# Attention into two expert layers on one core: softplus of the first two steps and two weight loads listed with the attention, the inverse root in 8 instructions, and new orders where the second layer changes group and ends

## The chip, the core and the metric

One core of a Trainium2 chip runs the whole program. Its engines have their own instruction streams: TensorE (PE, matrix products into PSUM), VectorE (DVE), ScalarE (ACT), GpSimd (POOL) and SyncE (SP, which issues the DMAs). An engine takes its instructions in the order in which the program lists them, and one that waits holds all that stands behind it. The metric is device time in microseconds of one execution, the median of several.

## The reference

Attention over 4 batches, 8 heads, 576 positions of 64, then an expert layer with softplus, then a gated one with a root mean square norm:

```
cum    = cumsum(max(s, 0))
scores = q k^T / 8 + min(-(cum_i - cum_j), 0), causal
x      = softmax(scores) v                      # to 2304 tokens x 512
h      = x @ w_in;  g = softplus(h);  x = g @ w_out         # d_ff 2048
xn     = x / sqrt(mean(x*x) + 1e-6) * rms_g
out    = (silu(xn @ w_gate) * (xn @ w_val)) @ w_out2        # d_ff 1536
```

q, k, v, s and rms_g are 32-bit floats; the weight matrices arrive as 64-bit floats.

## The kernel before

Every product that needs 32-bit accuracy is done as three matmuls of a high and a low part (hi x hi, hi x lo, lo x hi). A high part is a rounded copy made by ScalarE; the low part is what is left, a subtraction on VectorE or GpSimd. A 64-bit weight chunk of 128 x 512 is loaded (`w_fetch`, L227, tile raw), and turned into 32 bits by ScalarE (`w_conv_a`, L238), VectorE (`w_conv_d`, L245 to L249) and GpSimd (`w_conv_p`, L261), then split.

The attention runs in 16 pairs of heads. It is written as a list of small operations with engines, durations and dependences (`attention_ops`); `attention_order` picks them greedily by a table of ranks (OFF), and the order so found is that of every engine. At its end stand the last pairs' products with v (V0, V1, Z0, Z1, L552), the copies of their results (O0 to O2, `a_ox`, L590, tile xz), their way over memory and the division (BC on SyncE, XM on GpSimd, XW on SyncE, tile x, L614), and H0 and H1, the first two `m1_h` of the next layer.

The first expert layer (m1) runs in 96 steps: 6 tiles of 384 tokens by 16 chunks of d_ff. Step i has 12 matmuls into h (`m1_h`, L792 to L794), softplus twice on ScalarE (`m1_sp`: l, L813, and its rounded copy gh, L814), the low part on VectorE (`m1_gl`, gl, L818) and 12 matmuls into four banks y (`m1_y`, L830). TensorE's order is h(i+2), Y(i), h(i+3), Y(i+1). The other instructions are put at positions in units of a step (`at`, tables OFF1 and OFF2) and sorted. After a tile's last step its y is added to what was stored (`m1_evac`, L845), squared and summed (`m1_ss`: squares on ScalarE, L863, sums on GpSimd, L865), and the inverse root is made by `m1_inv` (L885): an integer seed and three Newton steps of three VectorE instructions each (L894, L896, L898) for all 384 tokens on 128 partitions; GpSimd then multiplies (L902). The sixth tile's inverse root lies in the second layer's first part.

The second layer (m2) runs in 36 calls of `m2_g`: 3 groups of 768 tokens by 12 chunks of d_ff (f = 0 to 11). Each call makes the products of a Strassen-Winograd scheme, named by their weight form and token form, in this order: A12 B21 (bank D), A11 B11 (bank A), S2 T2 (A), S1 T1 (D), S3 T3 (A), S4 B22 (D), A22 T4 (A). Each is six matmuls of 384 columns (L979 to L981). Between them stand two halves of nine matmuls of 512 columns of the chunk before (`m2_out`, L1071). What reads a bank between two products holds the next one that writes it: c1 (L1011), u2 (L1030), m5 (L1038) on ScalarE, vB (L1047) and gB (L1049) on VectorE. The token forms of a new group (tile xf) are split by `n_split`: the copy on ScalarE (L968), the subtraction (L970) on VectorE for one half of them and on GpSimd for the other. This is done in the last call of a group (B21, B11, T2) and in the first call of the next (`fresh`: T1, T3, B22, T4). There the six output banks of the old group are also copied (`m2_evac`, L1082 on ScalarE, L1084 on VectorE) and stored; three in the first call and three in the second one. `m2_end` does the last chunk.

Of the kernel before, what the change touches and what calls it, by code (L numbers as in the profile page):

```python
# [115 lines left out]
    "H0": -23.02,  # L116
    "H1": -64.43,
# [28 lines left out]
def attention_moe_kernel(ctx, tc, q, k, v, s, w_in, w_out, w_gate, w_val, w_out2, rms_g, out):  # L146
# [470 lines left out]
    def attention_ops():  # L617
# [90 lines left out]
        for i in range(2):  # L708
            op((f"H{i}", 0), "PE", 2.1, lambda i=i: m1_h(i),
               [(f"X{a}", 0) for a in range(KD)] + [("MT", NP - 1), ("CL", NA - 1), ("CP", len(CONV) - 1)] + [("R" + x, p) for x in "abcd" for p in (NP - 2, NP - 1)], NP, mode="f")  # L710
# [98 lines left out]
    def m1_sp(i):  # L809
        h = st.pop(("h", i))  # L810
        l = st["l", i] = m1_tile("l", 2)
        gh = st["gh", i] = m1_tile("gh", 3, F32R)
        nc.scalar.activation(out=l, in_=h, func=AF.Softplus)  # L813
        nc.scalar.activation(out=gh, in_=h, func=AF.Softplus)  # L814

    def m1_gl(i):
        gl = st["gl", i] = m1_tile("gl", 3, F32R)
        nc.vector.tensor_tensor(out=gl, in0=st.pop(("l", i)), in1=f32(st["gh", i]), op=ALU.subtract)  # L818
# [66 lines left out]
    def m1_inv(t, k):  # L885
# [4 lines left out]
        if k == 0:  # L890
            nc.vector.tensor_scalar(out=z.bitcast(I32), in0=ms.bitcast(I32), scalar1=-0.5, scalar2=1597463007.0,
                                    op0=ALU.mult, op1=ALU.add)
        elif k % 3 == 1:
            nc.vector.tensor_tensor(out=w, in0=z, in1=z, op=ALU.mult)  # L894
        elif k % 3 == 2:
            nc.vector.scalar_tensor_tensor(out=w, in0=w, scalar=-0.5, in1=ms, op0=ALU.mult, op1=ALU.mult)  # L896
        else:
            nc.vector.scalar_tensor_tensor(out=z, in0=w, scalar=1.5, in1=z, op0=ALU.add, op1=ALU.mult)  # L898
# [62 lines left out]
    def n_split(g, j, nm):  # L961
# [7 lines left out]
        eng = nc.gpsimd if g > 0 and i % 2 else nc.vector  # L969
# [22 lines left out]
    def m2_g(n, fill=None):  # L992
# [18 lines left out]
        act(out=c1, in_=A, func=AF.Copy)  # L1011
        if n:
            m2_hi(n - 1, 1)
            m2_lo(n - 1, 1)
        tt(out=gA, in0=D, in1=c1, op=ALU.add)
        act(out=s0, in_=gA, func=AF.Sigmoid)
        tt(out=s0, in0=gA, in1=s0, op=ALU.mult)
        if f == 1 and g > 0:
            m2_evac(g - 1, 1)
        if n:  # L1020
            m2_out(n - 1, 0)
        else:
# [8 lines left out]
        renew(fresh, "B22")  # L1031
# [55 lines left out]
    def m2_end():  # L1087
        n = NS2 - 1
        m2_out(n - 1, 1)
        m2_hi(n, 1)  # L1090
        m2_lo(n, 1)
        m2_out(n, 0)
        m2_evac(NG - 1, 0)
        m2_out(n, 1)
        m2_evac(NG - 1, 1)


    with tc.manual_schedule():
# [22 lines left out]
        with ExitStack() as es0:  # L1121
# [27 lines left out]
            for v in sorted({STEPS[i][0] for i in NS}):  # L1149
# [17 lines left out]
                for a in range(KD):  # L1167
                    at(e + OFF2["ss"] + OFF2["sr"] * a, m1_ss, t, a)
# [5 lines left out]
                for k in range(10):  # L1174
# [60 lines left out]
```

## Time and profile before

| | us |
|---|---|
| median of 3 runs (1060.23 to 1061.2) | 1060.93 |
| the profiled execution | 1059.71 |
| its span, from the first to the last instruction | 1057.9 |
| TensorE busy | 1029.3 (97%) |
| VectorE busy | 693.4 (66%) |
| GpSimd busy | 570.0 (54%) |
| ScalarE busy | 540.6 (51%) |

The attention takes roughly the first 221 us of the span, the first expert layer the next 400, the second one the rest. A row of the timeline gives the start, the busy time of a group of like instructions, the engine, the line, the operation, what it writes and reads, and in brackets the engine's idle time just before with what ended it. A matmul shows as busy from its start to its modelled end, and the next one starts before that end.

### The profile page before, as it was taken

How to read it: one execution, taken by the hardware profiler on the slowest of the kernel's cores; microseconds unless marked ns; L12 is line 12 of the kernel's file. 1: busy time of each engine (PE TensorE's matmuls, PEld its weight loads, DVE VectorE, ACT ScalarE, POOL GpSimd, SP SyncE). 2: the span in 40 equal slices, each digit the busy share in tenths (PEclk: the TensorE clock that was granted, in tenths of full speed). 3: DMA queues.
4: the chain of work that ended last, by engine and by line, in shares of the span. 5: the costliest groups of instructions: out<-in, count | busy, mean ns of one | idle time of the engine just before them, and what ended most of it. 6: DMA issues, size and time to landing. Idle time of an engine off the chain costs nothing.

```text
span 1057.9 us, 19448 instructions
## 1 busy us (share of the span) xinstructions
PE 1029.3 (97%) x7212; PEld 953.8 (90%) x7212; DVE 693.4 (66%) x1141; ACT 540.6 (51%) x1189; POOL 570.0 (54%) x477
## 2 busy tenths in 40 slices
PE   6999999999999999999999999999989999899997
PEld 5788877889999999999989998999979999799997
DVE  8888988418776756889898654545664346734444
ACT  2455666536656544544544544445554445644443
POOL 4378878736766433555767245355453433644331
PEclk9999999999999999999999999999999999999999
DMA  8367664345555575766542323224242233333221
GB/s 155 78 161 172 166 164 134 106 133 159 173 154 161 184 257 179 231 230 194 146 151 84 117 81 98 70 86 161 88 130 71 81 121 104 99 100 89 86 70 60
DMA packets 143758, 139.68 MB, mean 132 GB/s; under 512 B 68656, under 2 KB 118960, under 8 KB 143664
## 3 DMA queue, kind: packets, MB, share of 16 engines
q1 hardware_dynamic: 143632, 138.44, 44.5%
q8 instruction: 57, 0.93, 0.4%
q14 instruction: 37, 0.30, 0.1%
q0 software_dynamic: 32, 0.00, 0.0%
HBM read 106.73 MB, written 31.53 MB: 131 GB/s over the span
## 4 chain that ended last, share of the span: by engine, by line
PE 60%; DVE 7%; issue 3%; POOL 3%; DMA 2%; ACT 2%; SPq 0%; POOLq 0%; ACTq 0%; DVEq 0%
PE y L830 12%; PE o L1071 10%; PE A L979 4%; PE A L981 4%; PE A L980 4%; PE D L981 3%; PE D L979 3%; PE D L980 3%; PE h L792 3%; PE h L794 3%; PE h L793 3%; PE x L1071 2%; PE x L792 1%; PE x L794 1%; PE x L793 1%
## 5 line engine op out<-in xcount | busy, mean ns | idle before, releaser
L925 POOL TENSOR_TENSOR w<-wl,w 128x512 fp32r<-128x512 f32 x108 | 140.1, 1313 | 211.7 <-ACT w L924 211.7
L1071 PE MATMUL o<-w,gg 128*128 128x512 f32 x540 | 153.3, 393 | 0.3
L830 PE MATMUL y<-gh,w 128*128 128x384 f32 x768 | 149.8, 335 | 2.9 <-ACT gh L814 1.7
L830 PEld LDWEIGHTS y<-gh,w 128*128 128x128 f32 x768 | 134.4, 188 | 4.5 <-ACT gh L814 2.0
L1071 PEld LDWEIGHTS o<-w,gg 128*128 128x128 f32 x540 | 100.8, 188 | 19.4 <-ACT yt L1082 0.9
L979 PE MATMUL A<-xf,w 128*128 128x384 f32 x288 | 97.2, 338 | 6.2 <-DVE l L1047 4.7
L980 PE MATMUL A<-xf,w 128*128 128x384 f32 x288 | 96.9, 336 | 0.7 <-DVE xf L970 0.7
L981 PE MATMUL A<-xf,w 128*128 128x384 f32 x288 | 97.0, 337 | 0.0
L1047 DVE TENSOR_TENSOR l<-A,gh 128x384 f32<-128x384 f32 x36 | 20.0, 556 | 115.8 <-ACT w L924 113.3
L535 ACT ACTIVATE e<-t 128x448 f32<-128x448 f32 (+2 forms) x128 | 56.4, 505 | 71.3 <-PE t L528 66.4
L818 DVE TENSOR_TENSOR gl<-l,gh 128x384 fp32r<-128x384 f32 x96 | 79.3, 831 | 16.1 <-ACT gh L814 16.0
L261 POOL TENSOR_TENSOR wf<-ur 128x512 int32<-128x512 int32 x44 | 62.6, 1424 | 50.4 <-DVE ur L249 36.2
L485 DVE TENSOR_REDUCE mc<-s 128x2 f32<-128x512 f32 (+4 forms) x160 | 76.3, 534 | 19.0 <-PE s L470 15.0
L792 PE MATMUL h<-xh,w 128*128 128x384 f32 x256 | 85.6, 335 | 0.0
L793 PE MATMUL h<-xl,w 128*128 128x384 f32 x256 | 85.5, 334 | 0.0
L794 PE MATMUL h<-xh,w 128*128 128x384 f32 x256 | 85.5, 334 | 0.0
L830 PE MATMUL y<-gl,w 128*128 128x384 f32 x384 | 82.4, 335 | 2.3 <-DVE gl L818 2.2
L245 DVE TENSOR_SCALAR ur<-ur 128x512 f32<-128x512 f32 x68 | 51.3, 754 | 35.2 <-ACT ur L238 35.2
L979 PE MATMUL D<-xf,w 128*128 128x384 f32 x216 | 72.9, 338 | 0.0
L981 PE MATMUL D<-xf,w 128*128 128x384 f32 x216 | 72.8, 337 | 0.0
L980 PE MATMUL D<-xf,w 128*128 128x384 f32 x216 | 72.5, 336 | 0.0
L261 POOL TENSOR_TENSOR w<-ur 128x512 int32<-128x512 int32 x24 | 34.8, 1451 | 68.7 <-DVE ur L249 48.1
(171 smaller groups left out, 2662.8 us busy)
## 6 DMA issues: line engine op xcount, KB each, us to landing
wl<-wf SPq DMA_DIRECT2D x108, 256.0 KB
raw<-in_moe_w_out_dram SPq DMA_DIRECT2D x28, 512.0 KB
wf<-w SPq DMA_DIRECT2D x24, 512.0 KB
raw<-in_moe_w_in_dram SPq DMA_DIRECT2D x16, 512.0 KB
raw<-in_moe_w_gate_dram SPq DMA_DIRECT2D x12, 512.0 KB
raw<-in_moe_w_val_dram SPq DMA_DIRECT2D x12, 512.0 KB
xr<-x SPq DMA_DIRECT2D x28, 192.0 KB
qn<-in_q_dram SPq DMA_DIRECT2D x16, 288.0 KB
```

Of the source, the lines that this page charges most:

```text
L261: nc.gpsimd.tensor_tensor(out=w.bitcast(I32), in0=u, in1=r3, op=ALU.add)
L485: nc.vector.reduce_max(out=o, in_=x, axis=AX.X, negate=True)
L792: nc.tensor.matmul(o, wh, xh, start=start, stop=False)
L793: nc.tensor.matmul(o, wh, xl, start=False, stop=False)
L794: nc.tensor.matmul(o, wl, xh, start=False, stop=stop)
L818: nc.vector.tensor_tensor(out=gl, in0=st.pop(("l", i)), in1=f32(st["gh", i]), op=ALU.subtract)
L830: nc.tensor.matmul(y[m][:, 0:T], x[:, m * P:(m + 1) * P], r, start=first and x is w[0] and r is gh, stop=last and r is gl)
L925: nc.gpsimd.tensor_tensor(out=t[:, 1, 0:w], in0=src, in1=f32(t[:, 0, 0:w]), op=ALU.subtract)
L979: nc.tensor.matmul(o, wh[:, c], xh, start=first, stop=False, skip_group_check=True)
L980: nc.tensor.matmul(o, wh[:, c], xl, start=False, stop=False, skip_group_check=True)
L981: nc.tensor.matmul(o, wl[:, c], xh, start=False, stop=last, skip_group_check=True)
L1071: nc.tensor.matmul(st["o2"][m], x[:, m * P:(m + 1) * P], r, start=(f == 0 and k == 0), stop=(f == F2 - 1 and k == 2))
```

## The change

It has five parts.

Attention's end: H0 and H1 exchange their ranks and H1 follows H0. The softplus of both (SP0, SP1), their low parts (SG0, SG1) and two weight loads (FX, chunks 12 and 13) become operations of the attention's list. Their tiles come from pools that the attention has open.

Inverse root: the seed, then one Newton step and one step of third order, 8 instructions for 10. The two squares (k = 1 and 4) are ScalarE's; VectorE has the seed and five others. The sixth tile's squares of y are put into the second call of the second layer by hand.

Group changes: T1 is split at the end of the old group's last call, T3 right behind c1, both wholly on GpSimd; B22 wholly on VectorE, T4 one half on each, both right behind the silu. The six copies of the old group's banks are spread as (0, 1), (2), (3, 4) and (5), and VectorE has only banks 0 and 4 of them.

The first chunk's Y of the second layer's first call (`fill`) is put ahead of the sigmoid.

End: the last chunk's second half is finished before its first one, and the output banks are done one by one as 3, 4, 5, 0, 1, 2.

```
-    "H0": -23.02,
-    "H1": -64.43,
+    "H0": -64.43,
+    "H1": -23.02,
+    "SP0": -60.0,
+    "SP1": -60.0,
+    "SG0": -60.0,
+    "SG1": -60.0,
+    "FX": -60.0,
...
+               [(f"X{a}", 0) for a in range(KD)] + [("MT", NP - 1), ("CL", NA - 1), ("CP", len(CONV) - 1)] + [("R" + x, p) for x in "abcd" for p in (NP - 2, NP - 1)] + [("H0", 0)] * i, NP, mode="f")
+        for i in range(2):
+            op((f"SP{i}", 0), "ACT", 2.1 - 1.25 * i, lambda i=i: m1_sp(i), [(f"H{i}", 0)]
+               + [(f"E{x}{hd}", p) for x in "abcd" for hd in range(2) for p in (NP - 2, NP - 1)], NP)
+            op((f"SG{i}", 0), "DVE", 0.6, lambda i=i: m1_gl(i), [(f"SP{i}", 0)], NP)
+        for c in range(2):
+            op(("FX", c), "SP", 0.65, lambda c=c: w_fetch(1, NA + c), [("BC", NP - 1), ("CD", NA - 1)], NP)
...
     def m1_sp(i):
         h = st.pop(("h", i))
-        l = st["l", i] = m1_tile("l", 2)
-        gh = st["gh", i] = m1_tile("gh", 3, F32R)
+        if i < 2:
+            if "l01" not in st:
+                st["l01"] = pools["e"].tile([P, 2, 1600], F32, tag="e", name="l")
+                st["g01"] = pools["split"].tile([P, 4, S], F32R, tag="hl", name="g", bufs=3)
+            l, gh = st["l", i], st["gh", i] = st["l01"][:, i, 0:T], st["g01"][:, i, 0:T]
+        else:
+            l = st["l", i] = m1_tile("l", 2)
+            gh = st["gh", i] = m1_tile("gh", 3, F32R)
         nc.scalar.activation(out=l, in_=h, func=AF.Softplus)
         nc.scalar.activation(out=gh, in_=h, func=AF.Softplus)
 
     def m1_gl(i):
-        gl = st["gl", i] = m1_tile("gl", 3, F32R)
+        gl = st["gl", i] = m1_tile("gl", 3, F32R) if i > 1 else st["g01"][:, 2 + i, 0:T]
         nc.vector.tensor_tensor(out=gl, in0=st.pop(("l", i)), in1=f32(st["gh", i]), op=ALU.subtract)
...
-        elif k % 3 == 1:
-            nc.vector.tensor_tensor(out=w, in0=z, in1=z, op=ALU.mult)
-        elif k % 3 == 2:
-            nc.vector.scalar_tensor_tensor(out=w, in0=w, scalar=-0.5, in1=ms, op0=ALU.mult, op1=ALU.mult)
-        else:
-            nc.vector.scalar_tensor_tensor(out=z, in0=w, scalar=1.5, in1=z, op0=ALU.add, op1=ALU.mult)
+        elif k in (1, 4):
+            nc.scalar.activation(out=w, in_=z, func=AF.Square)
+        elif k in (2, 5):
+            nc.vector.scalar_tensor_tensor(out=w, in0=w, scalar=-0.1875 if k == 2 else 64.0 / 9.0, in1=ms, op0=ALU.mult, op1=ALU.mult)
+        elif k == 3:
+            nc.vector.scalar_tensor_tensor(out=z, in0=w, scalar=0.5625, in1=z, op0=ALU.add, op1=ALU.mult)
+        elif k == 6:
+            nc.vector.scalar_tensor_tensor(out=w, in0=w, scalar=-10.0 / 3.0, in1=w, op0=ALU.add, op1=ALU.mult)
+        else:
+            nc.vector.scalar_tensor_tensor(out=z, in0=w, scalar=5.0, in1=z, op0=ALU.add, op1=ALU.mult)
...
-        eng = nc.gpsimd if g > 0 and i % 2 else nc.vector
+        eng = nc.gpsimd if (g > 0 and i % 2 if pool is None else pool) else nc.vector
         eng.tensor_tensor(out=t[:, 1], in0=src, in1=f32(t[:, 0]), op=ALU.subtract)
...
-        def renew(go, *names):
+        def renew(go, *names, pool=(None, None)):
             if go:
                 for nm in names:
                     for j in range(2):
-                        n_split(g + ahead, j, nm)
+                        n_split(g + ahead, j, nm, pool[j])
+
+        def squares(k, *ks):
+            if n == k:
+                for a in ks:
+                    m1_ss(NTILE - 1, a)
 
         prod(D, n, "A12", "B21", True, True)
         prod(A, n, "A11", "B11", True, False)
         act(out=c1, in_=A, func=AF.Copy)
+        renew(fresh, "T3", pool=(1, 1))
         if n:
             m2_hi(n - 1, 1)
             m2_lo(n - 1, 1)
+        if f == 1 and g > 0:
+            m2_evac(g - 1, (5,))
         tt(out=gA, in0=D, in1=c1, op=ALU.add)
+        if n:
+            m2_out(n - 1, 0)
+        else:
+            fill()
+        if fresh:
+            m2_evac(g - 1, (0, 1))
         act(out=s0, in_=gA, func=AF.Sigmoid)
         tt(out=s0, in0=gA, in1=s0, op=ALU.mult)
-        if f == 1 and g > 0:
-            m2_evac(g - 1, 1)
-        if n:
-            m2_out(n - 1, 0)
-        else:
-            fill()
+        squares(1, 0, 1)
         renew(ahead, "B21", "B11")
-        renew(fresh, "T1", "T3")
+        renew(fresh, "B22", pool=(0, 0))
+        renew(fresh, "T4", pool=(0, 1))
...
-        renew(fresh, "T4")
+        squares(1, 2)
         if fresh:
-            m2_evac(g - 1, 0)
-        if n + 1 < NS2:
+            m2_evac(g - 1, (2,))
+        elif n + 1 < NS2:
             u_split(n + 1, (2, 3))
...
+        squares(1, 3)
+        if fresh:
+            u_split(n + 1, (2, 3))
+        if n == NS2 - 1:
+            tt(out=s1, in0=gB, in1=s1, op=ALU.mult)
+            tt(out=vB, in0=vB, in1=s1, op=ALU.mult)
...
-        m2_hi(n, 0)
-        tt(out=s1, in0=gB, in1=s1, op=ALU.mult)
-        m2_lo(n, 0)
-        tt(out=vB, in0=vB, in1=s1, op=ALU.mult)
-
-    def m2_out(n, h):
+        if n < NS2 - 1:
+            m2_hi(n, 0)
+            tt(out=s1, in0=gB, in1=s1, op=ALU.mult)
+            m2_lo(n, 0)
+            tt(out=vB, in0=vB, in1=s1, op=ALU.mult)
+        if fresh:
+            m2_evac(g - 1, (3, 4))
+        renew(ahead, "T1", pool=(1, 1))
...
-                if m % 2:
+                if m % 2 if g == NG - 1 else m not in (0, 4):
...
-        m2_out(n - 1, 1)
         m2_hi(n, 1)
         m2_lo(n, 1)
-        m2_out(n, 0)
-        m2_evac(NG - 1, 0)
-        m2_out(n, 1)
-        m2_evac(NG - 1, 1)
+        m2_hi(n, 0)
+        m2_lo(n, 0)
+        m2_out(n - 1, 1, (3, 4))
+        for m in (3, 4, 5, 0, 1, 2):
+            if m == 5:
+                m2_out(n - 1, 1, (5,))
+            m2_out(n, m // 3, (m,))
+            m2_evac(NG - 1, (m,))
...
-                    if (nm != "h" or i > 1) and (nm != "Y" or i + 1 < len(STEPS)):
+                    if (nm == "Y" or i > 1) and (nm != "Y" or i + 1 < len(STEPS)):
...
-                    at(x + OFF1[nm], fn, ph, c)
+                    if ph == 2 or c > NA + 1 or nm != "CF":
+                        at(x + OFF1[nm], fn, ph, c)
...
-                    at(e + OFF2["ss"] + OFF2["sr"] * a, m1_ss, t, a)
+                    if not x:
+                        at(e + OFF2["ss"] + OFF2["sr"] * a, m1_ss, t, a)
...
-                for k in range(10):
+                for k in range(8):
                     at(e + OFF2["iv" + x] + OFF2["in" + x] * (k + 1), m1_inv, t, k)
```

The list of ScalarE at the border between the attention and the first expert layer, before; l and gh are the softplus of a step, xz the attention's results on their way out, xh the next tokens' high part:

```order
L590 ACTIVATE xz<-x_4055 128x192 x2
L590 ACTIVATE xz<-o_4085 128x384
L590 ACTIVATE xz<-x_4094 128x192 x2
L590 ACTIVATE xz<-o_4111 128x384
L813 ACT_TABLE_LOAD
L813 ACTIVATE l<-h 128x384
L814 ACTIVATE gh<-h 128x384
L788 ACTIVATE xh<-xr 128x384
L813 ACTIVATE l<-h 128x384
L814 ACTIVATE gh<-h 128x384
L788 ACTIVATE xh<-xr 128x384
L813 ACTIVATE l<-x_4170 128x384
```

and of the changed kernel, from its table load on:

```order
L830 ACT_TABLE_LOAD
L830 ACTIVATE l<-h 128x384
L831 ACTIVATE g<-h 128x384
L595 ACTIVATE xz<-o_4033 128x384
L595 ACTIVATE xz<-o_4059 128x384
L595 ACTIVATE xz<-x_4045 128x192 x2
L830 ACTIVATE l<-h 128x384
L831 ACTIVATE g<-h 128x384
L595 ACTIVATE xz<-o_4091 128x384
L595 ACTIVATE xz<-x_4102 128x192 x2
L595 ACTIVATE xz<-o_4121 128x384
L799 ACTIVATE xh<-xr 128x384 x2
```

The softplus of step 0 stood behind every xz; now both of the first steps' softplus stand between them, and the table load ahead of all of them that are shown.

The list of VectorE in the first call of the last group, before; xf are split token forms, yt the copied output banks, `l<-A,gh` is vB and `gl<-gl` the silu:

```order
L1015 TENSOR_TENSOR gl<-D,gh 128x384
L1017 TENSOR_TENSOR gl<-gl 128x384
L970 TENSOR_TENSOR xf<-xs,xf 128x384 x3
L970 TENSOR_TENSOR xf<-acc,xf 128x384
L1084 COPY yt<-o 128x256 x4
L1047 TENSOR_TENSOR l<-A,gh 128x384
L1049 TENSOR_TENSOR gl<-D,gh 128x384
L1052 TENSOR_TENSOR gl<-A,gl 128x384
```

and now:

```order
L1044 TENSOR_TENSOR gl<-D,gh 128x384
L1122 COPY yt<-o 128x256 x2
L1052 TENSOR_TENSOR gl<-gl 128x384
L991 TENSOR_TENSOR xf<-xs,xf 128x384 x2
L991 TENSOR_TENSOR xf<-acc,xf 128x384
L1077 TENSOR_TENSOR l<-A,gh 128x384
L1079 TENSOR_TENSOR gl<-D,gh 128x384
L1088 TENSOR_TENSOR gl<-A,gl 128x384
```

Ahead of vB stood four splits and four copies; now it is three splits and two copies, and the copies stand ahead of the silu.

The list of GpSimd there, before; w are split weight forms, xf the token forms:

```order
L970 TENSOR_TENSOR xf<-xs,xf 128x384
L925 TENSOR_TENSOR w_11267<-wl,w_11267 128x512
L925 TENSOR_TENSOR w_11270<-xr,w_11270 128x256
L970 TENSOR_TENSOR xf<-xs,xf 128x384 x3
L925 TENSOR_TENSOR w_11371<-wl,w_11371 128x512
L925 TENSOR_TENSOR w_11374<-wl,w_11374 128x512
L970 TENSOR_TENSOR xf<-sq,xf 128x384
```

and now:

```order
L991 TENSOR_TENSOR xf<-xs,xf 128x384
L946 TENSOR_TENSOR w_11251<-wl,w_11251 128x512
L946 TENSOR_TENSOR w_11254<-xr,w_11254 128x256
L991 TENSOR_TENSOR xf<-xs,xf 128x384 x4
L991 TENSOR_TENSOR xf<-sq,xf 128x384
L946 TENSOR_TENSOR w_11373<-wl,w_11373 128x512
```

Three token forms, two weights and one token form (T4's) in a row have become four token forms and T4's with no weight between them.

## Rows read from the trace of the kernel before

**Rows 1.** the page, span, parts 1 and 2

```profile
span 1057.9 us, 19448 instructions
PE 1029.3 (97%) x7212; PEld 953.8 (90%) x7212; DVE 693.4 (66%) x1141; ACT 540.6 (51%) x1189; POOL 570.0 (54%) x477
```

**Rows 2.** timeline, TensorE, 224 to 227.5 us; start, us, group, count, idle before

```profile
224.81 1.67 PE L830 MATMUL y<-gh,w 128*128 128x384 f32 x8 [1.66 <-ACT gh L814]
226.31 0.85 PE L830 MATMUL y<-gl,w 128*128 128x384 f32 x4
227.01 0.33 PE L792 MATMUL h<-xh,w 128*128 128x384 f32 x1
```

**Rows 3.** timeline, ScalarE, 220 to 225 us

```profile
221.42 1.28 ACT L813 ACT_TABLE_LOAD   x1
```

**Rows 4.** timeline, SyncE, ScalarE and TensorE, 226 to 241 us

```profile
227.40 4.44 SPq L614 DMA_DIRECT2D x<-xz  x2
231.89 0.43 SPq L227 DMA_DIRECT2D raw<-in_moe_w_in_dram  x1
236.78 0.66 ACT L238 ACTIVATE ur<-raw 128x512 f32<-128x512 f32 x1 [6.62 <-DMA raw<-in_moe_w_in_dram]
239.62 0.96 PE L830 MATMUL y<-gl,w 128*128 128x384 f32 x4 [0.66 <-DVE gl L818]
```

**Rows 5.** busy time by stretch (us, then PE, PEld, DVE, ACT, POOL, clock, DMA)

```profile
484.00:556.00 72.00, 69.10 (x388) 66.80 (x387) 65.19 (x84) 35.74 (x75) 49.25 (x38) 1.00 0.53 166
```

**Rows 6.** timeline, TensorE, 494 to 549 us

```profile
495.14 0.79 PE L830 MATMUL y<-gl,w 128*128 128x384 f32 x3 [0.71 <-DVE gl L818]
503.61 0.62 PE L830 MATMUL y<-gh,w 128*128 128x384 f32 x2 [0.73 <-DVE yt L845]
539.68 0.79 PE L830 MATMUL y<-gl,w 128*128 128x384 f32 x3 [0.88 <-DVE gl L818]
547.35 1.28 PE L830 MATMUL y<-gh,w 128*128 128x384 f32 x3 [0.44 <-DVE yt L845]
```

**Rows 7.** VectorE by line and shape, 300 to 640 us; busy us, mean ns

```profile
L896 DVE SCALAR_TENSOR_TENSOR sh<-sh,sq 128x384 f32<-128x384 f32 x15 | 12.0, 802 | 0.3
L894 DVE TENSOR_TENSOR sh<-acc 128x384 f32<-128x384 f32 x15 | 11.1, 738 | 0.2
```

**Rows 8.** timeline, ScalarE and TensorE, 636 to 640 us

```profile
636.22 0.53 ACT L863 ACTIVATE acc<-yt 128x384 f32<-128x384 f32 x1 [1.41 <-POOL yt L902]
639.28 0.45 PE L979 MATMUL A<-xf,w 128*128 128x384 f32 x1 [1.47 <-ACT gh L1011]
```

**Rows 9.** timeline, VectorE, TensorE, GpSimd and ScalarE, the group changes

```profile
769.26 3.64 DVE L970 TENSOR_TENSOR xf<-xs,xf 128x384 fp32r<-128x384 f32 x3 [0.27 <-ACT xf L968]
774.39 1.41 DVE L1084 COPY yt<-o 128x256 f32<-128x256 f32 x4
775.72 0.54 DVE L1047 TENSOR_TENSOR l<-A,gh 128x384 f32<-128x384 f32 x1
771.67 0.45 PE L980 MATMUL A<-xf,w 128*128 128x384 f32 x1 [0.39 <-DVE xf L970]
776.41 0.41 PE L979 MATMUL A<-xf,w 128*128 128x384 f32 x1 [2.34 <-DVE l L1047]
783.85 0.47 PE L1071 MATMUL x<-w,gg 128*128 128x512 f32 x1 [0.31 <-DVE yt L1084]
919.02 0.41 PE L979 MATMUL A<-xf,w 128*128 128x384 f32 x1 [2.37 <-DVE l L1047]
770.13 2.36 POOL L970 TENSOR_TENSOR xf<-xs,xf 128x384 fp32r<-128x384 f32 x2 [0.22 <-PE o L1071]
773.41 0.65 ACT L1082 ACTIVATE yt<-o 128x256 f32<-128x256 f32 x2
```

**Rows 10.** timeline, SyncE, the end

```profile
1049.61 0.81 SPq L1085 DMA_DIRECT2D out_dram<-gl  x2
1054.45 0.90 SPq L1085 DMA_DIRECT2D out_dram<-yt  x2
```

More of the change, by code (lines that the diff above doesn't have):

```diff
@@ L709, in attention_ops @@
             op((f"H{i}", 0), "PE", 2.1, lambda i=i: m1_h(i),
-               [(f"X{a}", 0) for a in range(KD)] + [("MT", NP - 1), ("CL", NA - 1), ("CP", len(CONV) - 1)] + [("R" + x, p) for x in "abcd" for p in (NP - 2, NP - 1)], NP, mode="f")
+               [(f"X{a}", 0) for a in range(KD)] + [("MT", NP - 1), ("CL", NA - 1), ("CP", len(CONV) - 1)] + [("R" + x, p) for x in "abcd" for p in (NP - 2, NP - 1)] + [("H0", 0)] * i, NP, mode="f")
[5 more added lines that the diff above has]
+            op(("FX", c), "SP", 0.65, lambda c=c: w_fetch(1, NA + c), [("BC", NP - 1), ("CD", NA - 1)], NP)
         for o in ops:
@@ L959, in attention_moe_kernel, with n_split @@
     FORMS = ("B21", "B11", "T2", "T1", "T3", "B22", "T4")
-    def n_split(g, j, nm):
+    def n_split(g, j, nm, pool=None):
         i = FORMS.index(nm) + 7 * j
@@ L1014, in m2_g @@
             m2_lo(n - 1, 1)
+        if f == 1 and g > 0:
+            m2_evac(g - 1, (5,))
         tt(out=gA, in0=D, in1=c1, op=ALU.add)
-        act(out=s0, in_=gA, func=AF.Sigmoid)
-        tt(out=s0, in0=gA, in1=s0, op=ALU.mult)
-        if f == 1 and g > 0:
-            m2_evac(g - 1, 1)
         if n:
@@ L1023, in m2_g @@
             fill()
+        if fresh:
+            m2_evac(g - 1, (0, 1))
+        act(out=s0, in_=gA, func=AF.Sigmoid)
+        tt(out=s0, in0=gA, in1=s0, op=ALU.mult)
+        squares(1, 0, 1)
         renew(ahead, "B21", "B11")
-        renew(fresh, "T1", "T3")
+        renew(fresh, "B22", pool=(0, 0))
+        renew(fresh, "T4", pool=(0, 1))
         if n == N5:
@@ L1030, in m2_g @@
         act(out=u2, in_=A, func=AF.Copy)
-        renew(fresh, "B22")
         if n + 1 < NS2:
@@ L1053, in m2_g, with m2_out @@
         st["lt", n, 0], st["lt", n, 1] = s0, vB
-        m2_hi(n, 0)
-        tt(out=s1, in0=gB, in1=s1, op=ALU.mult)
-        m2_lo(n, 0)
-        tt(out=vB, in0=vB, in1=s1, op=ALU.mult)
-    def m2_out(n, h):
+        if n < NS2 - 1:
[6 more added lines that the diff above has]
+        renew(ahead, "T1", pool=(1, 1))
+    def m2_out(n, h, ms=None):
         f = n % F2
@@ L1064, in m2_out @@
         gh, gl = st["g", n]
-        ms = range(3 * h, 3 * h + 3)
+        ms = range(3 * h, 3 * h + 3) if ms is None else ms
         jobs = [(m, k) for k in range(3) for m in ms]
-        if n == NS2 - 1:
-            jobs = [(m, k) for m in ms for k in range(3)]
         for m, k in jobs:
@@ L1072, in m2_out, with m2_evac @@
                              stop=(f == F2 - 1 and k == 2))
-    def m2_evac(g, h):
+    def m2_evac(g, ms):
         W = DM // 2
-        for m in range(3 * h, 3 * h + 3):
+        for m in ms:
             r = 2 * T * g + m * P
```

## The prediction

> **What bounds the kernel now.** The page's busy shares come first: TensorE 97% of the span, no other engine above 66% [rows 1]. So the kernel is bound by the matmuls, and only what makes TensorE wait, or what lies ahead of its first and behind its last matmul, is worth time. The number of matmuls does not change. The second view is TensorE's timeline, read for rows with idle time in brackets. What such a row costs is worked out so: four matmuls of 384 columns take 0.85 us, one takes 0.33 [rows 2], so they start 0.173 apart (0.52 by 3) and each one's modelled end lies 0.16 behind the next one's due start. A bracket of 1.66 is therefore 1.82 us lost. Third, for each such row, the timeline of the engine that the bracket names, to see what it did instead.
>
> **The attention's end.** The first Y waits 1.66 for gh, so 1.82 is lost [rows 2]. ScalarE spent 1.28 us of that on the table load [rows 3], ahead of the first softplus and behind the last xz. In the new list the load and both softplus pairs lie between the products with v, while TensorE has two or more microseconds of work that needs none of them; I count the 1.82 as gone. The second loss, 0.66 + 0.16 = 0.82, is a late gl [rows 4]: the weight load was issued at 231.89, behind the stores and loads of x that held SyncE's queue for 4.44 us from 227.40, ScalarE waited 6.62 us for it and VectorE's gl stood behind the conversion. The new list has both loads ahead of the last x; they leave about 4.4 us earlier, and the last x goes out 2 x 0.43 later, which nothing waits for at once. Together -2.64; that H0 and H1 are now apart adds changes between the two kinds of products, so -2.6. Bounds: -0.8 (only the load helps, and the softplus of step 0, which now stands ahead of xz, holds the products with v) and -3.0.
>
> **The inverse root.** Per tile VectorE does 10 instructions: the seed and three each at about 0.74, 0.80 and 0.80 [rows 7], the third line like the second, 7.0 us beside the seed. After: the seed and five of the 0.80 kind, 4.0. So VectorE is relieved of 3.0 us per tile, and ScalarE gets two squares of 0.53 [rows 8], 1.06. Where this matters is one stretch: from 484 to 556 VectorE is busy 65.19 of 72 us and TensorE only 69.10 [rows 5], and four waits there are VectorE's [rows 6]: 0.87, 0.89, 1.04 and, at 547.35, 0.60 and 0.60 more inside (three matmuls in 1.28 where 0.68 is due), 4.0 in all. Two tiles' roots lie in the stretch, so VectorE gets 6 us less work in it, more than each of the waits. Elsewhere its relief is hidden behind TensorE. I take -3.0. Bounds: -4.0 and -1.0, the second because the squares wait for VectorE and then hold the softplus behind them on ScalarE, and because GpSimd's share of the work slips with it.
>
> The Trainium skill, page "ScalarE: Activation LUTs", section "Rules for kernel authors", speaks against this part: simple elementwise work such as a multiplication belongs on VectorE, which is the faster there. The rows show a square at 0.53 us on ScalarE and the multiplication that it replaces at a mean of 0.74 on VectorE [rows 7, 8], so in this stretch the trace does not agree. By the rule alone the part would be worth the instructions saved, 2 x 0.80 per tile, and about -1.6 instead of -3.0.
>
> **The second layer's first calls.** A wait of 1.47 for c1, so 1.63 lost [rows 8]: ScalarE stood in front of c1 with squares of the sixth tile that waited for GpSimd. They are put behind the silu now, and the inverse root before them ends earlier: -1.6 (bounds -1.0 and -1.6). The sixth tile's own second square now stands on ScalarE ahead of a c1 that TensorE needs soon: +0.3, up to one Square of 0.53.
>
> **The group changes.** At the first, A22 waits 2.34 for vB, 2.50 lost; S3 waits 0.39, 0.55 lost; at the next call a bank's copy costs 0.31 and 0.26 of overlap, 0.57 [rows 9]. That is 3.6, and the second change repeats all three (its A22 is the row at 919.02): 7.2. VectorE's row explains the first two: three splits took 3.64, a fourth and four copies (1.41) followed, and vB itself only 0.54. In the new list ahead of vB stand three splits and two copies, one split and 0.7 of copies less, and the copies are done before the silu. Worked through from the rows: the silu ends at about 769.0 now (769.26 less the 0.27 of idle time) and need not end later, since the two copies fit in front of it while VectorE waits for the sigmoid; the three splits end at 769.0 + 3.64 = 772.7 at the slow rate, vB 0.54 later at 773.2. S3's second matmul, were nothing late, is due at 771.12, and A22 eleven matmuls behind it at 773.0. So 0.2 remains, and S4 may wait 0.1 to 0.3 for m5, because ScalarE has four split copies and one output copy (0.65 [rows 9]) ahead of u2 and m5. The copy of bank 5 at the next call is alone. I take -3.1 per change, -6.2. Bounds: -2.0 (the splits run at the slow rate throughout and GpSimd's last, T4's second half, comes late) and -3.6.
>
> The slow rate is worth a look: 3.64 / 3 = 1.21 per split, while GpSimd ran two of its own in 2.36 at the same time [rows 9]. The Trainium skill, page "SBUF — State Buffer", section "SBUF: two separate sides", has VectorE instructions with two SBUF inputs and GpSimd's share one pair of ports as an exclusive lock, so that the loser waits for the whole of the other's instruction. If so, five GpSimd splits in a row would hold each of VectorE's three for 1.18 + 0.55, 5.2 us, vB would end at 774.8, 1.8 behind A22's due time, and the changes would give -2 x 1.8 instead. The row bears the lock out in kind, but 1.21 a split is less than that sum, so I keep the row.
>
> **The end.** SyncE issues twelve stores from 1049.61 to 1055.35, one every 0.48 [rows 10]; the issues, not the matmuls, set the end. The last chunk's second half is now finished first, and the first bank can be stored after three matmuls: about 0.5 earlier, with a wait of TensorE of 0.6 before. -0.5; bounds -1.0 and +0.7 (the last bank's copy waits for TensorE or for a free tile).
>
> **The sum.** -2.6 - 3.0 - 1.6 + 0.3 - 6.2 - 0.5 = -13.6. On the profiled execution, 1059.71 (its span of 1057.9 and 1.8 around it), that is 1046.1. That execution lies 1.22 below the median of the runs, 1060.93, so the predicted median is 1047.3.
>
> **Rivals.** First, a smaller gain: the waits move to the next reader. VectorE and GpSimd hold each other at the group changes as in the bound (-4.0 for both), the squares give back two of the three microseconds, the border gives -0.8: with the others as forecast -0.8 - 1.0 - 1.3 - 4.0 - 0.5 = -7.6, a median of 1053.3. For it: 1.21 per split, and that every reordered list here is a queue in which the first wait holds all. Against: each of the waits has one named cause that the list removes. Chance 0.17.
>
> Second, all of it goes: -2.64 - 4.0 - 1.6 - 7.2 - 1.0 = -16.4, a median of 1044.5. For it: VectorE has slack of 6 us in the stretch of 4 us losses. Chance 0.13.
>
> Third, slower, by one mechanism: the squares on ScalarE. Twelve of them (two in each of six tiles) stand in a list in front of xh, softplus and conversion, and each waits for an instruction of VectorE, which is 90% busy in the stretch of [rows 5]. If each held ScalarE for as long as the longest wait for VectorE that the rows show, 2.34, and TensorE with it, that is 28 us, and the sum ends at 1075. It decides from 1.1 us per square. Against it: between h(i) and Y(i) lie 48 matmuls, 48 x 0.173 = 8.3 us, so a softplus late by two microseconds is not felt. Chance 0.04.
>
> Fourth, no change: the border and the group changes only move their waits (0.03).
>
> **Chances.** Forecast 0.63, the first two rivals 0.17 and 0.13, slower 0.04, none 0.03. What a measurement can tell from no change is about 0.2%, 2.1 us. Faster by more 0.93, within it 0.03, slower 0.04. The range of 8 in 10 takes in the second rival and most of the first: 1044.0 to 1054.0.
>
> **What would show it.** Right: no bracket at TensorE's first Y and none at A22 behind the group changes over 0.5; the first raw load of the layer issued near 227.5; VectorE under 61 us busy in the stretch that now has 65.19, and TensorE's waits there below 1.5 together; no wait for c1 near 639. Wrong: TensorE waits for S4's m5 or S3's T3 in the place of A22; TensorE waits for gh behind a square; u2 and m5 late by a microsecond. The prediction as a whole is wrong if the brackets on TensorE past the attention add up to over 8 us, or if a stretch that the change does not touch gets longer.

## The result and the profile after

The changed kernel takes 1046.33 us (median of 4, 1045.9 to 1046.97), the kernel before 1060.58 in the same comparison: a ratio of 0.9866, 95% interval 0.9849 to 0.9883. The prediction was 1047.3, range 1044.0 to 1054.0.

The page of the changed kernel, span and busy times [rows 1]:

```profile
span 1043.9 us, 19444 instructions
PE 1026.1 (98%) x7212; PEld 953.3 (91%) x7212; DVE 670.3 (64%) x1111; ACT 547.0 (52%) x1205; POOL 570.6 (55%) x479
```

The matmuls are as many as before, and the span is 14.0 us shorter. Where these 14.0 us lie is read from the timeline's start of the same matmul in both profiles:

| stretch of TensorE's work | before, us | after, us | difference |
|---|---|---|---|
| start to h(2) | 220.79 | 221.65 | +0.86 |
| h(2) to the first Y | 4.02 | 2.20 | -1.82 |
| first Y to the second layer | 399.04 | 394.68 | -4.36 |
| its calls 0 to 10 | 127.23 | 125.84 | -1.39 |
| calls 11 to 13 (first group change) | 38.90 | 35.51 | -3.39 |
| calls 14 to 22 | 103.71 | 103.59 | -0.12 |
| calls 23 to 25 (second change) | 38.90 | 35.52 | -3.38 |
| calls 26 to 34 | 103.70 | 103.51 | -0.19 |
| the last call to the end | 21.65 | 21.42 | -0.23 |

The first row is no effect that these runs can tell: in the thirteen profiles of kernels with nearly the same attention h(2) began between 219.7 and 222.6 us.

The timelines at the border, ScalarE, TensorE, SyncE and ScalarE again [rows 2 to 4]:

```profile
209.91 1.28 ACT L830 ACT_TABLE_LOAD   x1
217.94 0.48 ACT L831 ACTIVATE g<-h 128x384 fp32r<-128x384 f32 x1
223.85 2.24 PE L847 MATMUL y<-g,w 128*128 128x384 f32 x12
228.35 0.44 SPq L232 DMA_DIRECT2D raw<-in_moe_w_in_dram  x1
234.38 0.67 ACT L243 ACTIVATE ur<-raw 128x512 f32<-128x512 f32 x1 [5.30 <-DMA raw<-in_moe_w_in_dram]
```

The table load and both softplus pairs lie among the last products with v, Y's twelve matmuls have no bracket, and the first load is issued at 228.35, 3.5 us earlier than before; its data are there at 234.38, only 2.4 us earlier. Counted from h(2), which began 0.86 us later, that is 4.4 and 3.3.

The busy times of the crowded stretch [rows 5]: first in 72 us that begin 5 us earlier than before, then between the two matmuls that started at 484.04 and 556.05 before, which is the same work of TensorE:

```profile
479.00:551.00 72.00, 70.94 (x407) 70.06 (x406) 61.62 (x78) 39.14 (x83) 50.11 (x40) 1.00 0.54 176
481.96:550.73 68.77, 67.71 (x387) 66.83 (x387) 58.45 (x74) 37.17 (x78) 48.22 (x38) 1.00 0.52 167
```

And what is left of its waits [rows 6]; TensorE, ScalarE (a square of the inverse root, and the conversion behind it), VectorE:

```profile
535.43 0.96 PE L847 MATMUL y<-gl,w 128*128 128x384 f32 x4 [1.04 <-DVE gl L835]
522.73 0.52 ACT L911 ACTIVATE sh<-acc 128x384 f32<-128x384 f32 x1 [4.60 <-DVE acc L908]
523.58 0.65 ACT L243 ACTIVATE ur<-raw 128x512 f32<-128x512 f32 x1
524.33 0.72 DVE L250 TENSOR_SCALAR ur<-ur 128x512 f32<-128x512 f32 x1 [1.69 <-ACT ur L243]
```

VectorE is relieved: 61.62 for 65.19 us in 72, and 58.45 for 65.2 in the same work. But a square waited 4.60 us on ScalarE for its seed, and VectorE afterwards waited 1.69 us for the conversion behind that square. Of the four waits one of 1.04 for gl is left, and 0.29 us at a copy of y.

The first group change, GpSimd, VectorE, ScalarE, TensorE [rows 9]:

```profile
758.54 4.90 POOL L991 TENSOR_TENSOR xf<-xs,xf 128x384 fp32r<-128x384 f32 x4
761.98 0.74 DVE L1122 COPY yt<-o 128x256 f32<-128x256 f32 x2
763.78 1.02 DVE L991 TENSOR_TENSOR xf<-xs,xf 128x384 fp32r<-128x384 f32 x2
764.72 1.37 DVE L991 TENSOR_TENSOR xf<-acc,xf 128x384 fp32r<-128x384 f32 x1
766.19 0.56 DVE L1077 TENSOR_TENSOR l<-A,gh 128x384 f32<-128x384 f32 x1
764.23 0.47 ACT L1061 ACTIVATE gh<-A 128x384 f32<-128x384 f32 x1
764.75 0.44 PE L1000 MATMUL A<-xf,w 128*128 128x384 f32 x1 [0.32 <-ACT gh L1061]
```

GpSimd has finished T1 and T3 (758.54 + 4.90) before VectorE begins B22, whose two splits take 0.51 each instead of 1.21; only T4's, beside GpSimd's own, takes 1.37. vB follows the splits directly, A22 has no bracket. S3 now waits 0.32 for u2, which stands behind the four copies of B22 and T4 on ScalarE. The second change looks the same.

The end, TensorE and SyncE [rows 10]:

```profile
1033.96 1.09 PE L1109 MATMUL o<-w,gg 128*128 128x512 f32 x3 [0.49 <-ACT gg L1006]
1035.49 0.81 SPq L1123 DMA_DIRECT2D out_dram<-yt  x2
1040.43 0.89 SPq L1123 DMA_DIRECT2D out_dram<-gl  x2
```

The first store is issued at 1035.49, 12.99 us after the last call's start (before: 13.32), and the last group of issues ends 5.83 us behind the start of the first (before 5.74). TensorE now loses 0.66 us in the last chunk, before nothing.

### The profile page after: what moved, and what is told of

Read it like the earlier page. It is cut to its first block, busy times and chain, and to the rows that moved or that the text cites. A ratio compares the mean times of both kernels' runs of the same rounds, so it can differ in the third digit from the quotient of the medians.

```text
span 1043.9 us, 19444 instructions
## 1 busy us (share of the span) xinstructions
PE 1026.1 (98%) x7212; PEld 953.3 (91%) x7212; DVE 670.3 (64%) x1111; ACT 547.0 (52%) x1205; POOL 570.6 (55%) x479
## 4 chain that ended last, share of the span: by engine, by line
PE 87%; DVE 6%; ACT 2%; DMA 2%; POOL 1%; issue 1%; SPq 0%; ACTq 0%; DVEq 0%; POOLq 0%
PE y L847 15%; PE o L1109 11%; PE t L523 5%; PE A L1000 5%; PE A L1002 5%; PE A L1001 5%; PE s L467 4%; PE D L1000 4%; PE h L803 3%; PE D L1002 3%; PE h L805 3%; PE h L804 3%; PE D L1001 3%; PE o L557 3%; PE x L557 3%; PE x L1109 2%
## 5 line engine op out<-in xcount | busy, mean ns | idle before, releaser
L847 PE MATMUL y<-gh,w 128*128 128x384 f32 x752 | 145.9, 334 | 0.0
L847 PEld LDWEIGHTS y<-gh,w 128*128 128x128 f32 x752 | 131.6, 188 | 0.6 <-DVE yt L862 0.5
L835 DVE TENSOR_TENSOR gl<-l,gh 128x384 fp32r<-128x384 f32 x94 | 77.0, 827 | 19.0 <-ACT gh L831 18.9
```

The lines of the kernel that those rows point to most:

```text
L847: nc.tensor.matmul(y[m][:, 0:T], x[:, m * P:(m + 1) * P], r, start=first and x is w[0] and r is gh, stop=last and r is gl)
```

## The experiments

All are timed against the kernel before, and most differ from the changed kernel by one part. The code cuts are shortened; what stands behind a # in them is a note. Since whole-run intervals are about 2 us wide each way, the verdicts go by a stage's own loss: the starts of neighbouring matmuls, less the usual 0.173 or 0.231 us, summed where over 0.15 us.

| kernel | median, us | ratio to before, 95% | border | 470 us to layer 2 | calls 0 to 6 | change 1, 2 |
|---|---|---|---|---|---|---|
| before | 1060.58 | 1 | 2.65 | 4.46 | 1.83 | 3.93, 3.91 |
| changed | 1046.33 | 0.9866 (0.9849 to 0.9883) | 0 | 1.50 | 0.45 | 0.74, 0.76 |
| sq_vector | 1046.6 | 0.9862 (0.9841 to 0.9884) | 0 | 3.41 | 0.19 | 0.76, 0.75 |
| inv10 | 1048.89 | 0.9885 (0.9866 to 0.9904) | 0 | 4.72 | 0.20 | 0.74, 0.75 |
| sq_late | 1044.31 | 0.9835 (0.9815 to 0.9856) | 0 | 0 | 0.46 | 0.74, 0.75 |
| sq_late2 | 1044.83 | 0.9845 (0.9829 to 0.9861) | 0 | 0 | 0.46 | 0.75, 0.73 |
| halves | 1048.0 | 0.9876 (0.9861 to 0.9892) | 0 | 0.88 | 0.46 | 1.53, 1.53 |
| u2_first | 1044.36 | 0.9843 (0.9828 to 0.9857) | 0 | 1.88 | 0.46 | 0, 0 |
| both | 1042.61 | 0.9830 (0.9815 to 0.9845) | 0 | 0 | 0.46 | 0, 0 |
| copies_old | 1047.88 | 0.9874 (0.9858 to 0.9891) | 0 | 2.08 | 0.46 | 1.33, 1.34 |
| border_old | 1048.44 | 0.9879 (0.9865 to 0.9894) | 1.82 | 1.74 | 0.46 | 0.72, 0.73 |
| loads_old | 1050.04 | 0.9892 (0.9877 to 0.9907) | 2.67 | 1.90 | 0.46 | 0.73, 0.73 |
| soft_old | 1047.02 | 0.9862 (0.9846 to 0.9879) | 1.82 | 0.90 | 0.46 | 0.74, 0.73 |
| end_old | 1045.77 | 0.9853 (0.9836 to 0.9870) | 0.42 | 1.90 | 0.46 | 0.73, 0.73 |

The losses are of one profile each. The stretch from 470 us loses 0.88 to 2.08 in the eight kernels that don't touch its code, so a difference under about 1.2 us is not told apart there.

### Which part of the shorter root counts

The squares back on VectorE:

```
-            nc.scalar.activation(out=w, in_=z, func=AF.Square)
+            nc.vector.tensor_tensor(out=w, in0=z, in1=z, op=ALU.mult)
```

> The changed kernel (1046.33 us) with the two squares of each tile's inverse root on VectorE again (8 instructions as in the change, all on VectorE). Theory (load on VectorE decides): VectorE gets two of about 0.74 us more per tile; TensorE's waits for VectorE between 479 and 551 us grow from about 1.9 us to about 3, the time by 1.0 to 1.5 us, to 1047.3 to 1047.8. Rival (the squares hold ScalarE: it stands idle 4.60 and 3.73 us in front of two of them, with the conversion for VectorE behind): without them ScalarE's conversion comes earlier, VectorE is not starved, the waits fall below 1 us and the time by about 1 us, to 1045.3.

The loss rises to 3.41, by more than the theory said; the rival's fall did not come. The whole time does not show it (1046.6, single runs from 1044.51 to 1049.05). The loss in calls 0 to 6 falls by 0.26: that is the sixth tile's second square, which no longer stands ahead of a c1.

The ten instructions of before:

```
-                for k in range(8):
+                for k in range(10):   # with the three Newton steps on VectorE
```

> The changed kernel with the inverse root as before (ten instructions on VectorE, three Newton steps), all else as changed. Theory: the part is worth what the stretch from 479 to 551 us got back, 2.8 us: 1049.1, with waits of 0.8 to 1 us each for gl and yt as in the kernel before. Rival (the waits there came from the weight loads and the order at the attention's end, which now run some microseconds earlier): less than 1 us, 1046.3 to 1047.2.

The loss is 4.72, as before the change, with the same readers late. So the part is worth about 3.1 here (4.72 less 1.6, the mean of the eight). Of this 1.3 would be from two instructions less, little more than the variation, and 1.8 from the squares' move. The busy times between the same two matmuls, inv10 and sq_vector:

```profile
482.19:554.37 72.18, 68.85 (x387) 66.80 (x387) 64.33 (x83) 35.72 (x75) 48.91 (x38) 1.00 0.52 165
```

```profile
482.73:553.68 70.95, 68.14 (x387) 66.77 (x387) 61.43 (x78) 35.77 (x76) 49.17 (x38) 1.00 0.52 163
```

The squares and what follows later in the lists:

```
-   at(e + OFF2["iv" + x] + OFF2["in" + x] * (k + 1), m1_inv, t, k)
+   at(e + OFF2["iv" + x] + OFF2["in" + x] * (k + 1) + (0 if x else [0, .8, .8, .8, 1.3, 1.3, 1.3, 1.3][k]), m1_inv, t, k)
```

> The changed kernel with the squares and what follows them in the inverse root (tiles 1 to 5) put 0.8 steps later (first three) and 1.3 steps later (the other four), behind the conversion and the softplus that stood behind each square. Theory (squares hold ScalarE): ScalarE's idle time in front of a square falls from 4.6 to under 1.5 us, VectorE's wait for ScalarE's conversion of 1.69 us goes, the wait of 1.04 us for gl near 534 us goes: 1.0 to 1.5 us less, about 1045.1. Rival (VectorE's load decides): the wait stays and the time stays within 0.3 us of 1046.3, or it grows because the last multiplications come later.

The loss is gone, but this run leaves something out: the last steps had slipped behind two of each tile's four multiplications by the root, so these two read it unfinished, and the output is another one. So the same was done again with those steps ahead of the multiplications, at shifts of 0, 0.8, 0.8, 0.8, 1.15, 1.06, 0.84 and 0.62:

> The changed kernel with ScalarE's squares of the inverse root (tiles 1 to 5) behind the conversion and the softplus that stood behind them, and the last instructions of the root still ahead of the multiplications that read it. The run before this one had the same order on ScalarE, but two of each tile's four multiplications read the root before its last steps. Theory (a square that waits for VectorE holds ScalarE's conversion, for which VectorE waits in turn): TensorE's waits from 470 us to the second layer fall from 1.50 us to under 0.5; with 0.9 less elsewhere at most, 1044.5 to 1045.5 on the scale on which the changed kernel has 1046.3. Rival (the gain of the earlier run came from the multiplications that did not wait): the waits stay above 1 us, or return as waits for yt, whose multiplications now end later, and the time stays within 0.4 us of the changed kernel's.

The loss is again 0. ScalarE there (a conversion, the first square, the second), and the busy times, in 72 us and between the same two matmuls:

```profile
518.56 0.66 ACT L243 ACTIVATE ur<-raw 128x512 f32<-128x512 f32 x1
520.41 0.55 ACT L911 ACTIVATE sh<-acc 128x384 f32<-128x384 f32 x1
527.02 0.53 ACT L911 ACTIVATE sh<-acc 128x384 f32<-128x384 f32 x1 [0.51 <-DVE acc L915]
```

```profile
476.00:548.00 72.00, 72.00 (x417) 71.83 (x416) 65.06 (x79) 39.33 (x83) 51.91 (x41) 1.00 0.57 179
480.04:547.09 67.05, 67.05 (x387) 66.88 (x387) 60.18 (x74) 37.09 (x78) 48.51 (x38) 1.00 0.56 171
```

Counted from h(2), the conversion starts at 298.9 us here and at 301.9 in the changed kernel, where it stood behind the square; the squares wait 0 and 0.51 us. VectorE's busy share is that of the kernel before (65.06 of 72 us) and TensorE never waits. In the same work VectorE has 5.0 us less than before, but 1.7 more than the changed kernel (60.18 for 58.45), which lost 1.50. So between these two VectorE's load does not decide; the order of the lists does. Which list is not shown, for the run moved two things. On ScalarE the squares went behind the conversion; on VectorE the root's steps, which the table shifts with them, went behind a gl. The root's first multiplication and the gl next to it, in the changed kernel and in sq_late2:

```profile
527.13 0.55 DVE L913 SCALAR_TENSOR_TENSOR sh<-sh,sq 128x384 f32<-128x384 f32 x1
529.16 0.55 DVE L835 TENSOR_TENSOR gl<-l,gh 128x384 fp32r<-128x384 f32 x1
```

```profile
523.57 0.55 DVE L835 TENSOR_TENSOR gl<-l,gh 128x384 fp32r<-128x384 f32 x1
524.04 1.65 DVE L913 SCALAR_TENSOR_TENSOR sh<-sh,sq 128x384 f32<-128x384 f32 x1
```

The wait of 1.69 us for the conversion is longer than the wait of 1.04 that was left for gl, so the squares' place alone could account for it; but sq_vector, without any square on ScalarE and with 3.0 us more on VectorE in the same work, lost 3.41, so VectorE's own list can cost as much. A run that moves only one of the two was not made.

### The group changes

```
-        renew(fresh, "T3", pool=(1, 1))   # and so for B22, T4 and T1
+        renew(fresh, "T3")                # one half on VectorE, one on GpSimd
```

> The changed kernel with T1, T3, B22 and T4 split half on VectorE and half on GpSimd as before, at the new places. Theory (the places and the copies decide, not the engines, since VectorE has three splits ahead of vB in either): the same within 0.4 us, 1046.3, and no wait for vB over 0.5 us at the group changes. Rival (VectorE and GpSimd hold each other, so that pairing decides): VectorE's splits take 1.2 us each instead of the 0.5 of now, S3, S4 or A22 wait 0.5 to 1 us more at each of the two changes: 1047.3 to 1048.3.

Both were wrong on the way: it costs 0.8 per change, but neither vB nor slow splits in the first call make it. VectorE, ScalarE (the sigmoid), TensorE:

```profile
759.30 1.84 DVE L991 TENSOR_TENSOR xf<-xs,xf 128x384 fp32r<-128x384 f32 x2
762.17 0.53 ACT L1051 ACTIVATE gl<-gl 128x384 f32<-128x384 f32 x1 [1.68 <-DVE gl L1044]
764.78 0.44 PE L1000 MATMUL A<-xf,w 128*128 128x384 f32 x1 [1.10 <-ACT gh L1061]
```

The halves of T1 and T3 on VectorE, 1.84 us together, stand ahead of gA; the sigmoid waits 1.68 for gA, and with it all copies behind it up to u2, for which S3 waits 1.10.

```
-        renew(fresh, "T4", pool=(0, 1))        # ahead of S2
         act(out=u2, in_=A, func=AF.Copy)
+        renew(fresh, "T4", pool=(0, 1))
```

with the next weights' first copies behind m5 in that call.

> The changed kernel with T4's copies on ScalarE behind u2 at the group changes, and the next weights' copies behind m5. Theory (ScalarE's queue ahead of u2 and m5 makes the two waits of 0.48 and 0.26 us that are left at each change): both go, 0.74 per change, 1.5 us in all: 1044.9 on the scale on which the changed kernel has 1046.3. Rival (T4's second half on GpSimd, now later, makes A22 wait instead, or the next weights come late at the next call's A12): 0 to 0.5 us at most, 1045.8 to 1046.5.

Both losses are 0, as the theory had it. ScalarE's u2 and m5, and T4 on GpSimd, which still ends in time:

```profile
762.17 0.47 ACT L1060 ACTIVATE gh<-A 128x384 f32<-128x384 f32 x1
763.37 0.48 ACT L1068 ACTIVATE gh<-D 128x384 f32<-128x384 f32 x1
763.54 1.37 POOL L991 TENSOR_TENSOR xf<-sq,xf 128x384 fp32r<-128x384 f32 x1 [1.34 <-ACT xf L989]
```

The two improvements together:

> The two before this one together. They lie in different stages, so their gains add: theory 1.5 + 1.5 = 3.0 us, 1043.4 on the scale on which the changed kernel has 1046.3, and no wait of TensorE above 0.3 us between 300 us and the last chunk but those of the sixth tile. Rival: one of them moves its wait on, and the sum is 1 to 1.5 us.

1042.61, a ratio of 0.9830 (0.9815 to 0.9845) to the kernel before; the losses that are left from 300 us on are 0.46 by the sixth tile and 0.66 in the last chunk. The interval ends below that of the changed kernel (0.9849 to 0.9883), though the two were not timed side by side.

```
-        if fresh:
-            m2_evac(g - 1, (0, 1))    # ... (2,), (3, 4), (5,)
+            m2_evac(g - 1, (0, 1, 2)) # behind m5; (3, 4, 5) in the next call, odd on ScalarE
```

> The changed kernel with the old group's output banks copied as before: three behind m5 in the first call, three in the second, odd ones on ScalarE and even ones on VectorE, all else as changed. Theory of the prediction (four copies of 1.41 us ahead of vB were a part of the 2.50 us wait of A22): A22 waits about 0.7 us more and the next call's two waits of 0.30 and 0.57 us are back: +1.2 to 1.6 per change, 1048.7 to 1049.5 on the scale of 1046.3. Rival (the splits alone made the wait; the copies fit in idle time): only the 0.9 of the next call comes back or less, 1046.3 to 1048.1.

It costs 0.6 per change in losses over 0.15 (24.87 us from call 12 to call 14 for 23.98), a wait of A22 for vB behind four copies; VectorE, then TensorE's A22:

```profile
766.92 1.40 DVE L1118 COPY yt<-o 128x256 f32<-128x256 f32 x4
768.25 0.54 DVE L1075 TENSOR_TENSOR l<-A,gh 128x384 f32<-128x384 f32 x1
768.85 0.44 PE L1000 MATMUL A<-xf,w 128*128 128x384 f32 x1 [0.42 <-DVE l L1075]
```

The next call's waits did not come back. In this run the copies of the next call stand ahead of gA and not behind the silu, so it does not restore that place, and what removed the 0.87 there was not tried by itself.

### The border

```
-            op((f"SP{i}", 0), "ACT", ...)   # and SG, FX, the ranks and H1 behind H0
+            at(i + OFF1[nm], fn, i)         # from the first layer's positions, as before
```

> The changed kernel with the attention's end as before: H0 and H1 with their old ranks, the first two softplus, their low parts and the two weight loads placed by the first expert layer. Theory: the first Y waits 1.66 us for gh again and a gl near 239 us 0.66, 2.6 us in all: 1048.9 on the scale on which the changed kernel has 1046.3. From the first matmul of h(2) to the second layer's first one it should take about 2.6 us more than the changed kernel's 396.9, less or more what the stretch near 500 us varies by. Rival (H0 and H1 apart cost TensorE what the waits gave back, so that the layer only begins later): under 1.3 us.

> The changed kernel with only the two weight loads placed as before, behind the last loads of x on SyncE. Theory of the prediction (the late load makes gl late near 239 us): a wait of about 0.7 us there, 0.8 lost, and none at the first Y: 1047.1. Rival (the load came 3.5 us earlier but its data only 2.4 us, and there is slack, so the loads do not matter): no wait over 0.2 us near 239 us, 1046.3.

> The changed kernel with only the order of H0 and H1 and the place of their softplus as before, the two loads early as changed. Theory (the table load and the two softplus pairs stood between the last products and the first Y): the first Y waits about 1.7 us for gh, 1.8 lost, and no wait near 239 us: 1048.1. Rival (the first Y is late with the early softplus too, since TensorE's own products moved): under 0.5 us.

The timelines, border_old (TensorE's first Y, ScalarE's first conversion):

```profile
226.17 1.68 PE L835 MATMUL y<-gh,w 128*128 128x384 f32 x8 [1.66 <-ACT gh L819]
237.03 0.66 ACT L243 ACTIVATE ur<-raw 128x512 f32<-128x512 f32 x1 [5.49 <-DMA raw<-in_moe_w_in_dram]
```

loads_old (SyncE, ScalarE, TensorE):

```profile
232.54 0.43 SPq L232 DMA_DIRECT2D raw<-in_moe_w_in_dram  x1
237.02 0.66 ACT L243 ACTIVATE ur<-raw 128x512 f32<-128x512 f32 x1 [8.16 <-DMA raw<-in_moe_w_in_dram]
239.85 1.65 PE L845 MATMUL y<-gl,w 128*128 128x384 f32 x4 [2.19 <-DVE gl L833]
```

soft_old:

```profile
226.32 1.68 PE L837 MATMUL y<-gh,w 128*128 128x384 f32 x8 [1.66 <-ACT gh L821]
234.49 0.67 ACT L243 ACTIVATE ur<-raw 128x512 f32<-128x512 f32 x1 [2.80 <-DMA raw<-in_moe_w_in_dram]
```

loads_old undoes the loads alone and soft_old all but the loads. Without either part 1.82 is lost (2.65 in the kernel before), with the early loads alone still 1.82, and with the early softplus alone 2.67. The late load's data come at 236.8 to 237.0 whatever TensorE does, since SyncE holds the load behind x's way over memory. A gl waits when the first conversion begins more than about 11 us behind the first Y: 11.97 us before (0.82 lost), 10.86 in border_old (none), 13.39 in loads_old (2.67), 10.53 in the changed kernel (none). This is a rule of this kernel alone; the other runs fit it, with 11.02 in sq_vector (none) and 11.46 in end_old (0.42). The wait at the first Y hid the late load; taken away alone, it is paid at the next place. So soft_old came as expected, border_old 0.8 below it, and loads_old not at all: 0.8 was expected and 2.67 was lost.

### The end

```
-        m2_out(n - 1, 1, (3, 4))
-        for m in (3, 4, 5, 0, 1, 2):
...
+        m2_out(n - 1, 1)      # then hi and lo of half 1, m2_out(n, 0) and its copies,
+        m2_out(n, 1)          # and these; half 0 is finished in the last call
```

> The changed kernel with the last chunk as before (its first half first, the banks in order 0 to 5 and three matmuls of a bank together). Theory (SyncE's issues set the end): TensorE's wait of 0.49 us for gg goes and its last matmul is 0.7 earlier, but the first store is issued 0.5 us later against the rest, and the span ends 0.2 to 0.5 us later: 1046.5 to 1046.8. Rival (the changed end costs what it gives): the end comes 0.2 us earlier or more, 1046.1 or less.

SyncE's first and last issues in it:

```profile
1037.51 0.81 SPq L1121 DMA_DIRECT2D out_dram<-gl  x2
1042.35 0.89 SPq L1121 DMA_DIRECT2D out_dram<-yt  x2
```

TensorE's 0.66 of the last chunk are gone, as expected, and the first store is issued 13.28 us behind the last call's start, 0.29 later than in the changed kernel. From the last call's start to the end it is 21.60 us, in the changed kernel 21.42, in the kernel before 21.65; but kernels with the same end had 21.40 to 22.68, so a gain of 0.2 isn't told from none. The 0.42 at the border in this run comes from a late first conversion, and the edit does not touch that place.

## Why the prediction was right

The terms were -2.6, -3.0, -1.3, -6.2 and -0.5; by the stages they came at -2.65, -2.96, -1.39, -6.77 and -0.23, together -14.0 for -13.6. That the sum came so close is in part luck: the group changes gave 0.6 more and the end 0.3 less, and the root's term was mostly chance to the digit, since the same code lost anything from 0.88 to 2.08 there, which would give -2.4 to -3.6.

The border: -2.6 forecast, 2.65 to 0 measured. The total was right, its division was not: the terms 1.82 and 0.82 were added as if each edit earned its own, while loads_old shows that the early softplus alone gains nothing against the kernel before (2.67 for 2.65), and soft_old that the early loads alone gain 0.8 at most.

The inverse root: -3.0 forecast, 4.46 to 1.50 measured, -2.96. The reason was half right. VectorE's relief came as counted, 6.8 us in the same work for 6 forecast, and inv10 and sq_vector show that the loss comes back with its instructions. But the relief alone does not set the loss: sq_late2 has VectorE busier than the changed kernel and no wait. The bound that I gave (squares hold ScalarE) is seen at work in the waits of 4.60 and 1.69 us; sq_late2 gets back all of the 1.50 us, with VectorE's list changed too.

That hold is also the first half of the slower rival, and it came as large as the rival had it:

```profile
L911 ACT ACTIVATE sh<-acc 128x384 f32<-128x384 f32 x10 | 5.3, 526 | 28.1 <-DVE acc L908 17.5 <-DVE acc L915 10.6
```

ScalarE stood idle 28.1 us in front of the ten squares of tiles 1 to 5 (in sq_late2 4.0), the longest hold 4.60; 28 us were assumed. The second half, that TensorE loses as much, did not come: it lost 1.50 at most by them. I lay that to the 8.3 us between h and Y, which no run tested. "VectorE under 61 us busy", which I had named as a sign, came true in the same work (58.45), but it says little: sq_late2 has 60.18 and no loss, the changed kernel less and a loss.

On the Trainium skill's rule on multiplications (page "ScalarE: Activation LUTs", section "Rules for kernel authors"), sq_vector decides for this stretch: with the squares on VectorE it lost 3.41 us, with them on ScalarE 0.88 to 2.08, so here the trace does not agree. One square alone hardly tells: 0.53 us on ScalarE, on VectorE 0.55 in the median and up to 1.65. The page's reason is VectorE's speed in bf16, and these are 32-bit floats.

c1 in the first calls: -1.6 and +0.3 forecast, -1.39 in calls 0 to 10; sq_vector shows the +0.26 as the square's. inv10, with the old root, lost only 0.20 there, so the gain is not the shorter root's; it goes with the new places of the squares of y and of `fill`, which no run separates.

The group changes: -3.1 each forecast, -3.39 and -3.38 measured. The slow rate that I took for all three splits did not hold: B22's splits ran at 0.51 since GpSimd was through with T1 and T3. Of the Trainium skill's exclusive lock (page "SBUF — State Buffer", section "SBUF: two separate sides") the trace shows that VectorE's splits are slow, 1.21 to 1.37, only beside GpSimd's. Its result, -1.8 per change, was worked out for five GpSimd splits beside VectorE's three, and that did not come about: four of the five had ended at 763.44, before VectorE's first began at 763.78. So the changed kernel does not test it. The small waits for u2 and m5 were forecast in kind (0.3 to 0.5) and came at 0.74. copies_old gives the copies 0.6 to 0.9 of the gain, halves gives the engines of the splits 0.8, by the halves of T1 and T3 ahead of gA, which I had not seen. The rest, about half of the gain, goes with the new places of the splits, which every run kept; no run shows it by itself.

The end: -0.5 forecast, -0.23 measured, which is not told from none. The wait that was to be its price, 0.6, came at 0.66.

## What to carry to other kernels

Before two stalls in a row are added up, ask which clock the second one hangs on: if it is a transfer's own, removing the first alone moves the cost on. When two engines hand work to each other in order, a busy share of 90% says less than who stands behind whom: an instruction that waits is worth a try behind whatever the other engine needs next. Compare an engine's busy time between the same two matmuls, since equal windows hold unequal work. And a reader that opens a bank for the next product goes ahead of copies that have slack.

## What was not expected of the hardware

With nearly the same attention, h(2) began anywhere from 219.7 to 222.6 us, and from the last chunk to the end it took 21.40 to 22.68 us in kernels with the same code there; both are as large as the effects of single parts, and are why the stages and not whole times were compared.
